# An attention and mixture-of-experts kernel: nine first products of the last batch turned round, their result transposed by DMA, the output tile split, the order refitted

## The chip, the cores and the metric

The kernel runs on one core of one Trainium2 chip. The metric is the device time of one execution in microseconds; the kernel before takes 357.3 us, the median of three runs (356.98 to 357.76).

## The reference

Sliding-window attention with sink tokens feeds a dense mixture of four experts. Shapes: q, k and v are (4 batches, 8 heads, 768 tokens, 64); x has 3072 tokens of 512; w1 is (4, 512, 1024), w2 is (4, 1024, 512).

```python
keep = is_sink | in_window                 # 4 sinks, window 128
a = softmax(where(keep, q @ k.T / 8, -1e9))
x = (a @ v) as (tokens, heads * dim)
p = domain_probs / (domain_probs.sum(-1, keepdims=True) + 1e-09)
for e in range(E):
    h = np.maximum(x @ w1[e], 0.0)
    out += p[:, e:e + 1] * (h @ w2[e])
```

## The kernel before, in words

**Work and tiling.** Tokens are worked in groups g of 256, three to a batch b, twelve in all. Attention of a batch consists of scores (line 673), values (735) and a DMA transpose of the result to x with features on partitions (`xT`, issued from SP at line 775). The first product of a group and an expert, x times w1, is a *unit* (b, g, e). Its result, after ReLU and the gate p, is `H`, with hidden features on partitions. The second product, H times w2, gathers all four experts of a group in a PSUM accumulator (`emit_product`, line 1316).

**Seven products in place of eight.** Most units and all second products from the third group on use a scheme of seven half-size matrix products, P1 to P7, of sums and differences of quarter blocks. Sums of the weights are made once (`weight_form1`, `weight_form`), those of the tokens once for a group (`tokens`, line 1103, tile `T`), those of H once for a unit (`chore`, line 1235, tiles `S` and `H` itself). All of these are VectorE work.

**A fast unit** (`emit_fast`, line 1135) issues each of its seven products as 8 matmuls: a block of 128 x 128 of the weight form stands in the array and 128 tokens stream past it (line 1158). Three PSUM banks X, Y and V take them. ScalarE seeds Y with P1 (line 1204) and keeps P5 in SBUF as fp32 in the memory of one half of H (line 1217); VectorE adds twice (1211, 1226) and then gates the four quarters with ReLU times the gate (1191). As tokens lie along the free dimension there, the gate is a tile of 128 x 256 with the same row on all partitions, loaded by SP (`load_gate`, 457) in a ring of four buffers. A quarter goes to the second product directly, so H is complete when the four gates are done.

**What sets the order.** The kernel is unrolled by a planner that runs while it is built. It keeps a clock for each engine (`pe`, `act`, `dve`, `sp`, lines 113 to 219) and at each step picks, among the steps that are ready, the one of the lowest priority number (lines 1535 to 1564). Attention is 1.9 when due and 3 otherwise, a pair of scores 0.1 less, an open unit's next product 2, opening a second unit OPEN, a second product LOW_PRODUCT. At most WIDE = 2 units are open. `SHARE_OF` spreads a batch's attention over the work of the batches before. Evacuations are queued with a slack (`later`, 152), and the one with the earliest due time goes first; "any" lets ScalarE or VectorE take it, whichever is free first. `joins` (1546) keeps a new unit from opening while a pair of scores is due and at least HOLDS units are open. `widened` (975) gives three more H buffers out of qkT once all attention is done. Each engine runs its instructions in the planner's order and waits on semaphores for what isn't ready.

**The output tile.** `emit_product` collects a group's result in one tile `osb` of two halves of 128 tokens, with one buffer; each half goes to memory by a DMA of its own (lines 1383 and 1324). Late groups alternate between it and two `aT` buffers.

Of the kernel before, what the change touches and what calls it, by code (L numbers as in the profile page):

```python
# [9 lines left out]
ALU = mybir.AluOpType  # L10
# [6 lines left out]
def kernel(  # L17
# [40 lines left out]
    ]  # L58

    NGATE = 4  # L60
    FIRST = 1
    START = {0: (1, 0), 1: (0, 2), 2: (0, 0), 3: (1, 0)}
    MIX = 6
    SHARE_OF = (0.9, 0.79, 0.98)
    LEAD = (1.01, 1.0)
    DUE = 1.9
    LOW_PRODUCT = 2.3
    LOW_SECOND = 2.7
    HIGH_PRODUCT = 1.9
    EARLY = -0.01  # L70
    MASK = 4000
    GATE = 1500
    GATE0 = 900
    FORM = 6000
    TOKEN = 5000
    MARGIN = 0
    HOLD = 0
    FULL = 7
    STEP0 = 0.01
    READY = 40  # L80
    WIDE = 2
    OPEN = 2.2
    SOON = 34000
    NEARLY = 2
    ROWED = 24000
    GATED = 38000
# [1 line left out]
    ROWS1 = 1500  # L88
    ONACT = 1
    ONE = 2  # L90
    HOLDS = 1
    MORE = 2
    BOTH = 1
    PAIR = 0
    OVER = 4
    ALONE = 1.3
    BEHIND = 1500
    CHORES = 3
    BIASED = 1
    FAST = tuple(START)  # L100
    BZ = 0
# [45 lines left out]
    def take(i, until):  # L147
        ring[i] = until
# [299 lines left out]

    def load_gates():

        while len(gate_sb) < len(mix.order) and (
            len(gate_sb) < (NGATE if t["pe"] > GATED else FIRST) or mix.order[len(gate_sb) - NGATE] in mix.finished
        ):
            b, g, e = mix.order[len(gate_sb)]
            load_gate(b * NG + g, e)

    def load_gate(pair, e):
# [480 lines left out]
    class Mixture:  # L938


        def __init__(self):
            self.early = {g: list(range(E)) for g in range(NEARLY)}
            self.open = []
            self.units = []
            for b, g in PAIRS:
                fast = [e for e in range(E) if self.is_fast(b, g, e)]
                slow = [e for e in range(E) if e not in fast]
                if b == 0:
                    fast, slow = list(range(E)), []
                while fast or slow:  # L950
                    for x in (fast, slow):
                        if x:
                            self.units.append((b, g, x.pop(0)))
            self.order = list(self.units)
            self.T, self.T_at, self.fast, self.finished = {}, {}, {}, set()
            self.second, self.live, self.since, self.turn, self.credit = [], 0, 0, 0, 0.0
            self.H, self.H_at, self.H_part = {}, {}, {}
            self.S, self.S_at, self.waiting, self.last = {}, {}, [], []
            self.products = [(b, g, m) for b, g in PAIRS for m in CHAIN]
            self.piece, self.part, self.chores = 0, 0, 0  # L960
            self.at, self.S4_at, self.C22 = {}, {}, {}
            self.done = 0.0
            self.stored, self.homed = [], False
            self.spare, self.lent = [], {}

# [4 lines left out]
            return bool(self.open or any(self.early.values()) or self.units or self.second or self.products)  # L970

        def room(self):
            return self.spare or self.live < NH

        def widened(self):

            x = sb.tile([P, 2, NHP, S], BF16, name="qkT", tag="qkT", bufs=1)
            x = x.rearrange("p i h n -> p (i h n)")
            n = 2 * QF * 2 * P
            self.spare = [x[:, i * n:(i + 1) * n].rearrange("p (k f t n) -> p k f t n", k=2, f=QF, t=2) for i in range(3)]  # L980

        def opened(self, b, g, e):

            if self.spare:
                self.H[b, g, e] = self.spare.pop()
                self.lent[b, g, e] = self.H[b, g, e]
            else:
                self.H[b, g, e] = mo.tile([P, 2, QF, 2, P], BF16, name="H", tag="H", bufs=NH)
                self.live += 1
            fast = self.is_fast(b, g, e)  # L990

            def complete(at):
# [141 lines left out]

        def emit_fast(self, u, m, ready):
            b, g, e = u["unit"]
            H, part, at = self.H[b, g, e], self.H_part[b, g, e], u["at"]
            if m == "P1":
                spare = [i for i in range(6) if ring[i] <= ready + 40]
# [92 lines left out]
            else:  # L1232
                u["last"](end)

        def chore(self):
# [24 lines left out]
            b, g, e = u = self.waiting[0]  # L1260
            if any(x[:2] < (b, g) and x[2] == "P5" for x in self.products) or any(x[:2] < (b, g) for x in self.last):
                return False
            if (b, g) == PAIRS[0] and (len(self.stored) < 2 * NEARLY or self.stored[-1] > t["pe"] + 500):
                return False
            self.waiting.pop(0)
            if (b, g) not in self.S:
                self.S[b, g] = [mo.tile([P, E, QF, P], BF16, name=f"S{i}", tag=f"wide{i}", bufs=1) for i in range(2)]
            H = self.H[b, g, e]
            H11, H21, H22 = H[:, 0, :, 0], H[:, 0, :, 1], H[:, 1, :, 1]
            S = self.S[b, g]  # L1270
            steps = [(nc.vector.tensor_add, S[0][:, e], H21, H22), (nc.vector.tensor_sub, S[1][:, e], S[0][:, e], H11),
                     (nc.vector.tensor_sub, H21, H11, H21)]
# [43 lines left out]
        def emit_product(self):  # L1316
# [40 lines left out]
            if m == "P1":  # L1357
                late = not att.more() and ahead == B - 1
                if late and self.homed:
                    x2 = [sb.tile([P, 2, 4 * P], BF16, name="aT", tag="aT", bufs=4) for _ in range(2)]  # L1360
                    out_sb[b, g] = [i.rearrange("p h w -> p (h w)").bitcast(FP32) for i in x2]
                else:
                    x2 = mo.tile([P, 2, Dout], FP32, name="osb", tag="osb", bufs=1)
                    out_sb[b, g] = [x2[:, i] for i in range(2)]
                self.homed = late and not self.homed
                self.C22[b, g] = join(2, lambda at: store(at))
            o = out_sb[b, g]
# [41 lines left out]
        def emit_second(self):  # L1409
            ready = self.second_ready()  # L1410
            g, s, e = self.second.pop(0)
            if g not in out_sb:
                out_sb[g] = mo.tile([P, 2, Dout], FP32, name="osb0", tag=f"wide{g}" if g < 2 else "osb", bufs=1)
                if g == 0:
                    gates()
            dst = out_sb[g][:, s]
# [32 lines left out]
                    used.add(e)  # L1449

    idle_products(acc[1], 9)
    mix = Mixture()
# [26 lines left out]
    while mix.more() or att.more():  # L1481
# [46 lines left out]
            next_form()  # L1528
        if ahead + 1 < B and not att.more() and (ahead == 0 or (ahead + 1, 0) in turned_at) and (ahead == 0 or mix.done >= sum(work[:ahead]) * LEAD[ahead - 1]):
            ahead += 1  # L1530
            att = Attention(ahead)
            upto = mix.done
        share = (sum(work[:ahead]) - upto) * SHARE_OF[max(ahead - 1, 0)]
# [8 lines left out]
                opts.append((max(r, now), p, "att", step))  # L1542
        s2, p = mix.second_ready(), mix.product_ready()
        behind = max(t["dve"] - now, 0.0) + 500 * sum(x[2] == "dve" and x[0] < now + 300 for x in pend)
        opts.append((max(p, now), HIGH_PRODUCT if behind > BEHIND or mix.live >= FULL else LOW_PRODUCT, "product", None))
        joins = due and ahead >= PAIR and att.two() and not late and len(mix.open) >= HOLDS
        opts += [(max(f, now), p, "first", x) for f, p, x in mix.firsts() if not (joins and x[0] in ("unit", "early"))]
        opts.append((max(s2, now), 1 if mix.since >= 1 else LOW_SECOND, "second", None))
# [14 lines left out]
            continue  # L1563
        r, _, kind, step = min(opts, key=lambda o: (o[0] > now + 40, o[0] if o[0] > now + 40 else 0, o[1]))
        assert r < 1e11
        if kind == "att":
            att.emit(step)
        elif kind == "first":
# [41 lines left out]
```

## Time and profile before

| | before |
|---|---|
| time, median of 3 runs | 357.3 us (356.98 to 357.76) |
| the profiled execution's own time | 357.25 us |
| its span | 355.5 us |
| granted TensorE clock, mean | 0.998 |
| TensorE busy | 349.7 us, 4563 matmuls |
| VectorE busy | 305.9 us, 704 instructions |
| ScalarE busy | 165.2 us, 423 instructions |
| first products of fast units, L1158 | 2240 matmuls of 128 columns |
| second products, L1335 | some 1100 matmuls, most of 256 columns |

The profile is of one execution. The span runs from the first to the last instruction. PE is TensorE, PEld its weight loads, DVE VectorE, ACT ScalarE, POOL GpSimd, SP the engine that issues most DMAs. A line number with L is a line of the kernel before; `cps` are the PSUM banks of fast units, `acc` the accumulators of second products, `sps` the banks of scores. Matmuls overlap, and their listed length (219 ns for 128 columns) is longer than the distance between two starts.

### The profile page before, as it was taken

Reading aid. Unit: us, or ns where it says so; the run is one execution under the profiler, and the core shown is the slowest. Engines: PE = TensorE matmul, PEld = TensorE weight load, DVE = VectorE, ACT = ScalarE, POOL = GpSimd, SP = SyncE. Lnnn points to the kernel's source line nnn. Section 1 sums busy time; section 2 is a strip of 40 time slices with the busy share of each in tenths; the row PEclk is TensorE's granted clock in tenths of the full one; section 3 lists DMA queues with packets and bytes.
Section 4 is the critical chain, followed back from the end, with each engine's and each line's share of the span. In section 5 each row is a group of like instructions: output and inputs, shape, how many; then the busy total and the mean of one; then the engine's idle time right before and its main releaser. Section 6 shows DMA issues by size and latency. Waiting matters only on the chain.

```text
span 355.5 us, 10875 instructions
## 1 busy us (share of the span) xinstructions
PE 349.7 (98%) x4563; PEld 302.4 (85%) x4563; DVE 305.9 (86%) x704; ACT 165.2 (46%) x423; POOL 73.6 (21%) x91
## 2 busy tenths in 40 slices
PE   8999999999999999999999999999999999999996
PEld 3685769656789998998998999899899999999985
DVE  5885999978999999799698998799899899899740
ACT  5863724447884565554542345455464223322111
POOL 8955114230534306010340000000000000000000
PEclk9999999999999999999999999999999999999999
DMA  9999999999999999629999120310210211010011
GB/s 176 178 187 196 222 216 181 170 153 180 150 144 157 177 153 117 78 64 72 160 144 160 46 57 21 77 50 21 77 50 19 52 56 61 31 44 33 1 61 60
DMA packets 120125, 37.80 MB, mean 106 GB/s; under 512 B 101268, under 2 KB 116084, under 8 KB 120076
## 3 DMA queue, kind: packets, MB, share of 16 engines
q0 software_dynamic: 79104, 17.31, 57.7%
q1 hardware_dynamic: 39916, 19.28, 27.5%
q8 instruction: 35, 0.57, 0.7%
q10 hardware_dynamic: 1056, 0.52, 0.5%
q14 instruction: 14, 0.11, 0.1%
HBM read 40.98 MB, written 6.34 MB: 133 GB/s over the span
## 4 chain that ended last, share of the span: by engine, by line
PE 93%; DVE 3%; DMA 2%; ACT 1%; issue 0%; ACTq 0%; DVEq 0%
PE cps L1158 35%; PE acc L1335 33%; PE acc L1422 8%; PE hps L1071 7%; PE sps L692 3%; PE od L758 3%; DMA out_dram<-osb 2%; PE acc L568 1%; PE od L751 1%; DVE onat L788 1%; DVE aT L726 1%; PE tx L816 0%; DVE T L1127 0%; PE tr L589 0%; PE sinks L653 0%; ACT aT L717 0%
## 5 line engine op out<-in xcount | busy, mean ns | idle before, releaser
L1158 PEld LDWEIGHTS <-w 128*128 128x128 bf16 x1280 | 78.7, 98 | 2.9 <-issue 1.3
L1335 PEld LDWEIGHTS <-H 128*128 128x128 bf16 x684 | 63.5, 98 | 7.3 <-issue 1.1
L1191 DVE SCALAR_TENSOR_TENSOR H<-cps,gates 128x512 bf16<-128x512 f32 x96 | 64.1, 678 | 0.1
L1158 PEld LDWEIGHTS <-vf 128*128 128x128 bf16 x960 | 58.4, 98 | 1.0 <-issue 0.3
L717 ACT ACTIVATE aT<-sps 128x512 bf16<-128x512 f32 (+1 forms) x96 | 47.2, 574 | 16.6 <-PE sps L692 16.5
L1335 PE MATMUL acc<-w,H 128*128 128x256 bf16 x408 | 53.9, 273 | 0.0
L1158 PE MATMUL cps<-T,w 128*128 128x128 bf16 x640 | 48.9, 219 | 0.0
L1158 PE MATMUL cps<-xT,w 128*128 128x128 bf16 x640 | 47.6, 219 | 0.0
L1158 PE MATMUL cps<-T,vf 128*128 128x128 bf16 x640 | 46.2, 219 | 0.0
L797 ACT ACTIVATE onat<-od,R 128x64 bf16<-128x64 f32 x144 | 33.2, 320 | 21.2 <-DVE R L785 21.0
L1204 ACT COPY cps<-cps 128x512 f32<-128x512 f32 x40 | 23.2, 579 | 41.1 <-PE cps L1158 22.1
L1397 ACT COPY osb<-acc 128x256 f32<-128x256 f32 x35 | 13.1, 377 | 50.9 <-PE acc L1335 46.1
L1335 PEld LDWEIGHTS <-S 128*128 128x128 bf16 x320 | 30.1, 98 | 4.2 <-issue 1.0
L1071 PE MATMUL hps<-xT,w 128*128 128x256 bf16 x256 | 31.8, 273 | 0.1
L1211 DVE TENSOR_TENSOR cps<-H,cps 128x512 f32<-128x512 f32 x34 | 23.4, 689 | 8.3 <-PE cps L1158 4.3
L1422 PE MATMUL acc<-w,H 128*128 128x512 bf16 x128 | 29.9, 379 | 0.0
L305 POOL DMA_DIRECT2D vx<-in_v_dram x24 | 21.4, 908 | 39.6 <-PE od L758 28.9
L1335 PE MATMUL acc<-wf,H 128*128 128x256 bf16 (+1 forms) x208 | 28.4, 272 | 0.0
L1071 PEld LDWEIGHTS <-w 128*128 128x128 bf16 x256 | 24.2, 98 | 4.5 <-issue 0.7
L1226 DVE TENSOR_TENSOR H<-H,cps 128x512 f32<-128x512 f32 x34 | 23.1, 679 | 2.2 <-PE cps L1158 2.1
L1158 PE MATMUL cps<-xT,vf 128*128 128x128 bf16 x320 | 24.4, 219 | 0.0
L240 POOL DMA_DIRECT2D qkn<-in_q_dram x22 | 19.6, 893 | 22.3 <-DMA qkT<-qkn 14.7
(127 smaller groups left out, 526.7 us busy)
## 6 DMA issues: line engine op xcount, KB each, us to landing
w<-in_moe_w_dram POOLq DMA_DIRECT2D x6, 1024.0 KB, 18.5
out_dram<-osb SPq DMA_DIRECT2D x21, 256.0 KB
gates<-gate_rows SPq DMA_DIRECT2D x40, 128.0 KB
vx<-in_v_dram POOLq DMA_DIRECT2D x24, 128.0 KB, 7.7
qkn<-in_q_dram POOLq DMA_DIRECT2D x22, 128.0 KB, 6.9
qkn<-in_k_dram POOLq DMA_DIRECT2D x22, 128.0 KB, 7.1
w<-in_moe_w_dram POOLq DMA_DIRECT2D x4, 256.0 KB, 7.3
w<-in_moe_w_dram POOLq DMA_DIRECT2D x2, 512.0 KB, 11.0
```

Of the source, the lines that this page charges most:

```text
L240: nc.gpsimd.dma_start(out=both[:, i], in_=src[b, :, tb * P:(tb + 1) * P, :].rearrange("h p d -> p h d"),)
L305: nc.gpsimd.dma_start(out=vx[tb][:, :, 0:D], in_=v[b, :, tb * P:(tb + 1) * P, :].rearrange("h p d -> p h d"),)
L717: nc.scalar.activation(out=a[:, ph], in_=sps[ph][:, 0:w], func=AF.Exp, scale=scale)
L797: nc.scalar.mul(o[:, qi, hp, ph * D:(ph + 1) * D], od[:, qi, ph, 0:D], R[:, qi, ph])
L1071: nc.tensor.matmul(h[:, i].rearrange("p (q n) -> p q n", q=2), lhsT=w1_sb[e][:, db, fb * P:(fb + 1) * P], rhs=xT[b, g][:, :, db], start=(i ...
L1158: nc.tensor.matmul(y[:, f], lhsT=A[:, d, f * P:(f + 1) * P], rhs=T[:, d], start=(m in ("P1", "P5") and f == 0 and d == 0), stop=(d == 1), ...
L1191: nc.vector.scalar_tensor_tensor(out=dst, in0=src, scalar=0.0, in1=gate, op0=ALU.max, op1=ALU.mult)
L1204: nc.scalar.copy(out=tiles["Y"], in_=y)
L1211: nc.vector.tensor_add(tiles["V"], c5, tiles["X"])
L1226: nc.vector.tensor_add(c5, c5, y)
L1335: nc.tensor.matmul(y, lhsT=self.operand(b, g, e, m)[:, f], rhs=forms[e][m][:, f, cs], start=(k == 0 and f == 0 and m in (("P1", "P5", "P2" ...
L1422: nc.tensor.matmul(op, lhsT=H[:, fb // QF, fb % QF, s], rhs=w2_sb[e][:, fb, :], start=(fb == 0), stop=(fb == NFB - 1),)
```

## The change

Nine of the twelve units of the last batch, all but its first two and its last, are *turning*. Their tokens stand in the array and the weight form streams past, so each of the seven products is 2 matmuls of 512 columns and the result has tokens on partitions. The gate is then a scalar per partition: VectorE applies ReLU and gate in one instruction with a pointer operand, or ScalarE does it in two. Results go to half-buffers of 128 x 1024 bf16, and a DMA transpose from SP turns each into its half of H, two for a unit. Six half-buffers are taken from tiles that attention no longer needs, so turning units open only after attention's end. Gate tiles for these units are no longer loaded; a small table of the last batch's gates (128 x 6 x 4) is loaded and normalized once. The output tile becomes two tiles. The experts of the last group come in another order, and constants of the planner change.

```diff
+    TURN_ABOUT = 0
+    TURNED_UNITS = (2, 1)
+    EXPERTS = {(2, 2): (2, 0, 3, 1)}
-    SHARE_OF = (0.9, 0.79, 0.98)
+    SHARE_OF = (0.96, 0.92, 0.94)
-    LOW_PRODUCT = 2.3
+    LOW_PRODUCT = 2.7
-    MASK = 4000
-    GATE = 1500
-    GATE0 = 900
-    FORM = 6000
-    TOKEN = 5000
+    MASK = 5000
+    GATE = 800
+    GATE0 = 300
+    FORM = 8000
+    TOKEN = 3000
+    REST = 1500
+    LANDS = 0
-    OPEN = 2.2
-    SOON = 34000
+    OPEN = 2.5
+    SOON = 28000
-    HOLDS = 1
+    HOLDS = 2
-    CHORES = 3
+    CHORES = 4
...
+            mine = [u for u in self.order if u[0] == B - 1]
+            self.turning = set(mine[TURNED_UNITS[0]:len(mine) - TURNED_UNITS[1]])
+            self.gated = [u for u in self.order if u not in self.turning]
...
         def room(self):
+            if self.units and self.units[0] in self.turning and self.halves() < 2:
+                return False
             return self.spare or self.live < NH
...
+            for tag, bufs, n in (("qkn", NQB, 3), ("onat", 2, 2), ("aT", 4, 1)):
+                self.resting += [(t["pe"], sb.tile([P, QF, 2, P], BF16, name="rest", tag=tag, bufs=bufs)) for _ in range(n)]
...
+        def emit_turning(self, u, m, ready):
...
+                    def turned(k):
+                        def turn(at):
+                            nc.sync.dma_start(
+                                out=H[:, k].rearrange("c f t n -> c (f t) n"), in_=X[k].rearrange("p f t n -> p (f t n)"), transpose=True,
+                            )
+                            done = sp(at, issue=1330, takes=1400, turning=True) + LANDS
+                            self.H_part[b, g, e](done)
+                            self.H_part[b, g, e](done)
+                            self.resting.append((done, X[k]))
+                        return join(2, turn)
...
+            for d in range(2):
+                nc.tensor.matmul(
+                    y.rearrange("p f n -> p (f n)"), lhsT=T[:, d], rhs=A[:, d], start=(m in ("P1", "P5") and d == 0), stop=(d == 1), skip_group_check=True,
+                )
+            end = pe(2 * n, ready, n=2)
...
+            def gated(k, s, src, ready, slack, slot=None, then=None):
+                gate = own_gates[:, 2 * g + s, e:e + 1]
+
+                def run(engine):
+                    if engine == "act":
+                        nc.scalar.activation(out=src, in_=src, func=AF.Relu)
+                        act(n)
+                        nc.scalar.mul(X[k][:, :, s], src, gate)
+                        at = act(n)
+                    else:
+                        nc.vector.tensor_scalar(out=X[k][:, :, s], in0=src, scalar1=0.0, scalar2=gate, op0=ALU.max, op1=ALU.mult)
+                        at = dve(n, fixed=152)
...
+                later("any" if slot is not None else "dve", ready, slack, run)
...
+            if u in self.turning and self.H_at[u] > max(t["pe"], t["dve"]):
+                return False
...
-                    x2 = mo.tile([P, 2, Dout], FP32, name="osb", tag="osb", bufs=1)
-                    out_sb[b, g] = [x2[:, i] for i in range(2)]
+                    out_sb[b, g] = [mo.tile([P, Dout], FP32, name=f"osb{i}", tag=f"osb{i}", bufs=1) for i in range(2)]
...
+            if ahead == B - 2:
+                own_load()
+            elif ahead == B - 1:
+                own_made()
...
-        opts.append((max(p, now), HIGH_PRODUCT if behind > BEHIND or mix.live >= FULL else LOW_PRODUCT, "product", None))
+        opts.append((max(p, now), HIGH_PRODUCT if behind > BEHIND or mix.live >= FULL or wide and TURN_ABOUT and mix.turn_about else LOW_PRODUCT, "product", None))
```

`own_load` issues one DMA for the gate table, and `own_made` four small VectorE steps that normalize it. The seeds, the two additions and the banks of a turning unit are those of `emit_fast`; three of its four gates may go to ScalarE, and the fourth, whose source is the fp32 copy in SBUF, stays on VectorE.

More of the change, by code (lines that the diff above doesn't have):

```diff
@@ L449, in load_gates @@
     def load_gates():
-        while len(gate_sb) < len(mix.order) and (
-            len(gate_sb) < (NGATE if t["pe"] > GATED else FIRST) or mix.order[len(gate_sb) - NGATE] in mix.finished
+        while len(gate_sb) < len(mix.gated) and (
+            len(gate_sb) < (NGATE if t["pe"] > GATED else FIRST) or mix.gated[len(gate_sb) - NGATE] in mix.finished
         ):
-            b, g, e = mix.order[len(gate_sb)]
+            b, g, e = mix.gated[len(gate_sb)]
             load_gate(b * NG + g, e)
@@ L945, in __init__ @@
             for b, g in PAIRS:
-                fast = [e for e in range(E) if self.is_fast(b, g, e)]
+                fast = [e for e in EXPERTS.get((b, g), range(E)) if self.is_fast(b, g, e)]
                 slow = [e for e in range(E) if e not in fast]
@@ L954, in __init__ @@
             self.order = list(self.units)
+            mine = [u for u in self.order if u[0] == B - 1]
+            self.turning = set(mine[TURNED_UNITS[0]:len(mine) - TURNED_UNITS[1]])
+            self.gated = [u for u in self.order if u not in self.turning]
+            self.G, self.resting = {}, []
             self.T, self.T_at, self.fast, self.finished = {}, {}, {}, set()
@@ L961, in __init__ @@
             self.at, self.S4_at, self.C22 = {}, {}, {}
-            self.done = 0.0
+            self.done, self.turn_about = 0.0, False
             self.stored, self.homed = [], False
@@ L972, in room, with halves, half @@
         def room(self):
+            if self.units and self.units[0] in self.turning and self.halves() < 2:
+                return False
             return self.spare or self.live < NH
+        def halves(self):
+            return sum(x[0] <= t["pe"] + REST for x in self.resting)
+        def half(self):
+            return self.resting.pop(min(range(len(self.resting)), key=lambda i: self.resting[i][0]))[1]
         def widened(self):
@@ L990, in opened @@
             fast = self.is_fast(b, g, e)
+            if (b, g, e) in self.turning:
+                self.G[b, g, e] = [self.half(), self.half()]
             def complete(at):
@@ L1136, in emit_fast @@
             b, g, e = u["unit"]
+            if (b, g, e) in self.turning:
+                self.emit_turning(u, m, ready)
+                return
             H, part, at = self.H[b, g, e], self.H_part[b, g, e], u["at"]
@@ L1233, in emit_fast, with seed, both, run @@
                 u["last"](end)
+        def emit_turning(self, u, m, ready):
+            b, g, e = u["unit"]
+            H, X, at = self.H[b, g, e], self.G[b, g, e], u["at"]
+            n = QF * P
+            assert len(own_steps) == 4
+            if m in ("P1", "P5"):
+                spare = [i for i in range(6) if ring[i] <= ready + 40]
+                spare.sort(key=lambda i: (whole[i], ring[i]))
+                if m == "P1":
+                    assert len(spare) >= 2
+                    new = dict(X=spare[0], Y=spare[-1])
+                    u["unset"] = not whole[spare[-1]]
+                    u["slots"], u["tiles"] = {}, {}
+                    def turned(k):
[8 more added lines that the diff above has]
+                        return join(2, turn)
+                    u["turn"] = [turned(k) for k in range(2)]
+                else:
+                    new = dict(V=spare[0])
+                for name, i in new.items():
+                    u["slots"][name] = i
+                    u["tiles"][name] = bank(i, [P, QF, P], FP32, "cps", True)
+                    ring[i] = 1e12
+            slots, tiles = u["slots"], u["tiles"]
+            y = tiles[{"P1": "X", "P5": "V", "P6": "X", "P2": "Y", "P7": "X", "P3": "V", "P4": "X"}[m]]
+            A, T = forms1[e][m], self.T[b, g][m]
+            for d in range(2):
[3 more added lines that the diff above has]
+            end = pe(2 * n, ready, n=2)
+            self.done += 2 * n
+            if m == "P1" and u["unset"]:
+                w = w1_sb[e][:, 0]
+                nc.tensor.matmul(
+                    tiles["Y"].rearrange("p f n -> p (f n)"), lhsT=w[:, 0:P], rhs=w[:, 0:n], start=True, stop=True,
+                )
+                pe(n)
+            c5 = X[1].rearrange("p f t n -> p (f t n)").bitcast(FP32).rearrange("p (f n) -> p f n", f=QF)
+            def gated(k, s, src, ready, slack, slot=None, then=None):
[6 more added lines that the diff above has]
+                        at = act(n)
+                    else:
+                        nc.vector.tensor_scalar(out=X[k][:, :, s], in0=src, scalar1=0.0, scalar2=gate, op0=ALU.max, op1=ALU.mult)
+                        at = dve(n, fixed=152)
+                    if slot is not None:
+                        take(slot, at)
+                    u["turn"][k](at)
+                    if then:
+                        then(at)
+                later("any" if slot is not None else "dve", ready, slack, run)
+            if m == "P1":
+                u["last"] = join(2, lambda at: gated(1, 1, tiles["X"], at, GATE, slots["X"]))
+                def seed(engine):
+                    nc.scalar.copy(out=tiles["Y"], in_=y)
+                    at["P6"] = at["P2"] = act(n)
+                later("act", end, 0, seed)
+                at["P5"] = self.T_at[b, g]
+                def both(ready):
+                    def run(engine):
+                        nc.vector.tensor_add(tiles["V"], c5, tiles["X"])
+                        at["P7"] = at["P3"] = dve(n)
+                    later("dve", ready, 0, run)
+                u["both"] = join(2, both)
+            elif m == "P5":
+                def keep(engine):
+                    nc.scalar.copy(out=c5, in_=y)
+                    u["both"](act(n))
+                later("act", end, 0, keep)
+            elif m == "P6":
+                u["both"](end)
+            elif m == "P2":
+                gated(0, 1, y, end, GATE, slots["Y"])
+            elif m == "P7":
+                def run(engine):
+                    nc.vector.tensor_add(c5, c5, y)
+                    at["P4"] = dve(n)
+                    gated(1, 0, c5, at["P4"], 100, then=u["last"])
+                later("dve", end, 0, run)
+            elif m == "P3":
+                gated(0, 0, y, end, GATE, slots["V"])
+            else:
+                u["last"](end)
@@ L1412, in emit_second @@
             if g not in out_sb:
-                out_sb[g] = mo.tile([P, 2, Dout], FP32, name="osb0", tag=f"wide{g}" if g < 2 else "osb", bufs=1)
+                out_sb[g] = mo.tile([P, 2, Dout], FP32, name="osbw", tag=f"wide{g}", bufs=1)
                 if g == 0:
@@ L1449, in emit_second, with own_load, own_made, run @@
                     used.add(e)
+    own_gates = consts.tile([P, 2 * NG, E], FP32, name="own_gates")
+    own_sum = consts.tile([P, 2 * NG], FP32, name="own_sum")
+    own_steps = []
+    def own_load():
+        nc.sync.dma_start(out=own_gates, in_=moe_domain_probs[(B - 1) * S:].rearrange("(t p) e -> p t e", p=P))
+        sp()
+    def own_made():
+        steps = [
+            lambda: nc.vector.reduce_sum(out=own_sum, in_=own_gates, axis=AX.X),
+            lambda: nc.vector.tensor_scalar_add(out=own_sum, in0=own_sum, scalar1=1e-9),
+            lambda: nc.vector.reciprocal(out=own_sum, in_=own_sum),
+            lambda: nc.vector.tensor_mul(own_gates, own_gates, own_sum[:, :, None].to_broadcast([P, 2 * NG, E])),
+        ]
+        def run(engine):
+            steps.pop(0)()
+            dve(2 * NG * E)
+            own_steps.append(1)
+            if steps:
+                later("dve", t["dve"], 5000, run)
+        later("dve", t["pe"], 5000, run)
     idle_products(acc[1], 9)
@@ L1565 @@
         assert r < 1e11
+        mix.turn_about = kind == "first"
         if kind == "att":
```

## The prediction

> **What bounds the kernel now.** I read the shares of the page first, then the chain of waits in order of time, then the table of stretches, and last the timeline at the places where the chain leaves TensorE.
>
> ```profile
> PE 349.7 (98%) x4563; PEld 302.4 (85%) x4563; DVE 305.9 (86%) x704; ACT 165.2 (46%) x423; POOL 73.6 (21%) x91
> ...
> PE 93%; DVE 3%; DMA 2%; ACT 1%; issue 0%; ACTq 0%; DVEq 0%
> ```
>
> TensorE carries 93% of the chain that ended last. A busy PE may still hide waiting, so I took the spacing of matmul starts from unbroken pieces of the chain (start, length, what):
>
> ```profile
> 26.45 5.18 PE acc L1422 x24
> ...
> 304.63 5.36 PE cps L1158 x96
> ...
> 311.75 5.24 PE acc L1335 x48
> ...
> 331.19 20.11 PE acc L1335 x192
> ```
>
> 24 matmuls of 512 columns take 5.18 us, 0.216 each; 96 of 128 columns take 5.36 us, 0.0559 each; 48 of 256 take 5.24 us, 0.109 each. Setting every start in the trace against the spacing of its shape leaves 11.8 us that TensorE did not use: 6.2 us before 60 us, 5.6 us after it. From 280 us on there is none.
>
> ```profile
> 280.00:300.00 20.00, 20.00 (x294) 19.22 (x293) 19.63 (x42) 5.41 (x11) 0.00 (x0) 1.00 0.16 54
> 300.00:320.00 20.00, 20.00 (x274) 18.96 (x272) 18.38 (x39) 4.84 (x10) 0.00 (x0) 1.00 0.12 34
> ...
> 340.00:356.00 16.00, 12.19 (x128) 10.95 (x125) 2.69 (x7) 2.23 (x7) 0.00 (x0) 0.94 0.17 63
> ```
>
> The columns are PE, PEld, DVE, ACT, POOL, granted clock, DMA share and GB/s. Where the last batch runs, VectorE is nearly full too, ScalarE and the DMA engines are nearly free, and at the end VectorE has long stopped while TensorE works on. So only fewer TensorE nanoseconds, or fewer of the 11.8 us, shorten this kernel.
>
> **The turned products.** A product of a normal unit is 8 matmuls of 128 columns, 8 x 55.9 = 447 ns. A turned one is 2 of 512, 2 x 216 = 432 ns. Saved: 15.2 ns a product; 9 units of 7 products are 63, so **0.96 us**, all on the bounding engine. The weight loads fall from 8 to 2, but they are hidden already: 96 matmuls with as many loads start every 55.9 ns though one load is listed at 98 ns.
>
> The Trainium skill ("TensorE: Matmul & The Clock Gate", section on the back-to-back issue gap) gives a sustained spacing of about 81 ns at 128 columns and 131 ns at 512 in streams with weight loads. By it a product would fall from 648 to 262 ns and the change would win some 24 us; the chain above contradicts both figures.
>
> **VectorE and ScalarE.** The 36 gating instructions of these units leave their old form. Rows for the old and the new ones (busy, mean ns):
>
> ```profile
> L1191 DVE SCALAR_TENSOR_TENSOR H<-cps,gates 128x512 bf16<-128x512 f32 x96 | 64.1, 678 | 0.1
> ...
> L1086 DVE TENSOR_SCALAR H<-hps 128x512 bf16<-128x512 f32 x5 | 3.4, 685 | 0.5 <-PE hps L1071 0.4
> ...
> L1432 DVE TENSOR_SCALAR osb<-acc,scale_t 128x512 f32<-128x512 f32 x4 | 3.0, 750 | 3.4 <-PE acc L1422 3.4
> ```
>
> A scalar per partition seems to cost 65 ns (750 against 685), at most 36 x 0.07 = 2.5 us of VectorE. Against that, 27 of the 36 may go to ScalarE as two instructions of about 0.6 us each (606 for the ReLU of L1084, 579 for the copy of L1204): up to 27 x 0.60 = 16 us less VectorE, where 0.60 is its spacing in a row of such gates. ScalarE is a quarter busy there, so the cover is ample. I cost both at nothing, because TensorE has no wait from 280 us on and cannot have fewer than none. Without the cover, up to 2.5 us of VectorE work would be spread over a stretch with 2.0 us of VectorE idle (40 - 19.63 - 18.38), and 20 us of pure second products behind it would still absorb it. The four steps for the new gates on VectorE are tiny (0.16 to 0.18 us each by L925 and L928), and 24 numbers a partition are loaded some 100 us before use; nothing.
>
> **The DMAs.** Added are 18 transposes from SP, removed 9 gate loads. SP is held 1.24 us by a transpose (L775, 1237 ns undisturbed), so 22 us in some 55 us of queue; stores and the last gate loads stand behind them. From issue to the last landing record the undisturbed xT transposes, of the same 128 x 1024 size, took 3.03 us (221 us) and 3.08 us (250 us), and 3.66 us behind a gate load (275 us). The planner's book counts 1.33 + 0.8 + 1.4 + 0.9 = 4.43 us. A transposed half is thus ready 0.8 to 1.4 us ahead of plan; cost nothing. What waits for it is the second product on TensorE and the sums for P5 to P7 on VectorE. Each engine takes its instructions in the program's order, so a late landing would hold everything behind it on that engine. Under the heavier traffic of 159 to 190 us the same transposes took 5.3 to 8.3 us, the upper bound.
>
> The Trainium skill ("VectorE: DVE Perf Modes", section on the three transpose paths) lists 1309 ns for a 128 x 128 DMA transpose. Eight blocks one after another would be 10.5 us, twice the plan; the 3.03 us rows speak against it.
>
> **The output tile.** One stall in the chain is a copy that waits for a store of the same tile:
>
> ```profile
> 190.54 0.60 PE L1335 MATMUL acc<-qkn,S 128*128 128x256 bf16 x4
> ...
> 191.06 0.65 ACT L1397 COPY osb<-acc 128x256 f32<-128x256 f32 x2 [4.75 <-DMA out_dram<-osb]
> ...
> 191.48 0.60 PE L1335 MATMUL acc<-w,S 128*128 128x256 bf16 x4 [0.34 <-ACT osb L1397]
> ```
>
> Four matmuls end their slots at 190.54 + 0.44 = 190.98; the next starts at 191.48. The store was the second half's (L1324, 184.03, landed 6.99 us later); the copy writes the first half, whose store had landed long before. Two tiles remove that wait: **0.50 us**. Nothing else is late behind it: the timeline shows no wait of TensorE in the next microseconds.
>
> **The refitted order.** LOW_PRODUCT (2.3 to 2.7) and OPEN (2.2 to 2.5) keep their rank against each other and against the other priorities that can compete, so they change nothing. CHORES and the slacks reorder VectorE, whose order costs TensorE nothing after 280 us; before, I take zero with bounds. TOKEN acts early: four T steps hold 1.68 us of the chain at 14.7 to 16.5 us, so up to 0.7 us either way. SHARE_OF moves attention; what is lost after 60 us besides shape switches is about 1.2 us, the bound on both sides.
>
> HOLDS from 1 to 2 is more than a tuning. It kept a second unit from opening while a pair of scores was due; units open only while fewer than two are open, so at 2 the reservation never acts. A pair needs four free banks of six. What a lone group costs:
>
> ```profile
> 263.58 0.60 PE L1335 MATMUL acc<-w,H 128*128 128x256 bf16 x4
> ...
> 264.11 0.62 PE L692 MATMUL sps<-qkT 64*128 64x128 bf16 x12
> ...
> 264.66 0.62 PE L1158 MATMUL cps<-T,w 128*128 128x128 bf16 x8
> ```
>
> 264.11 is 0.09 us past the slots of the four before it, and another 0.09 follows the group: 0.19 us for each separate group. After 76 us there are 23 groups, some 12 of them pairs. Splitting none costs nothing, splitting all 12 costs 2.3 us. I take 2 (0.38 us), near the lower end: a ready pair still outranks a new unit (1.8 against 2.5), and pairs such as 264.11 stand where the open units were nearly done.
>
> **The sum.** On the profiled execution (357.25 us, span 355.5 and 1.7 around it; 0.05 below the median of 357.3): 357.25 - 0.96 - 0.50 + 0.38 = 356.17, so **356.2 us**.
>
> **Rivals.** *The forecast as worked out*, 355.3 to 356.8: 0.46. *The new order also recovers stalls* (1.2 us after 60 us, some of the 6.2 before): 354.2 to 355.3; for it, VectorE gains room; against it, TensorE waits for VectorE only early, where the new gates are not yet used: 0.16. *The pairs of scores come apart*, 6 to 12 of them: 357.25 - 1.46 + 1.1 to 2.3 = 356.9 to 358.1; for it, the reservation is gone and units fill banks; against it, the rank above: 0.20, mostly within 0.2%. *The turned halves come late*, the one on the slower side: each unit's first use stalls TensorE in order. It decides from 4.43 us after the gating; with 0.5 us of lateness for each of 9 units, 356.2 + 4.5 = 360.7, and slower than before from 0.2 us each. For it, two more hops (ScalarE, SP); against it, 0.8 to 1.4 us of reserve by the rows: 0.12. *The change does not do what it says*: half-buffers exist only once attention is done, so a third unit waiting for them, or early reshuffling, eats the gain (357 to 358.5). Before, the third unit of the last batch starts at 276.1 and the last attention transpose at 275.23, so there is little to wait for: 0.05. *Weight loads bind, not columns*: at 98 ns a matmul of 128 columns a turned unit would save 7 x (784 - 432) ns, 22 us in all, so 335; the 55.9 ns rows exclude it nearly: 0.01. The Trainium skill's spacing rule above points this way.
>
> **Numbers.** This kernel's measurement tells about 0.2% (0.7 us) from no change. Faster: 0.42 + 0.16 + 0.01 = 0.59. Within: 0.04 + 0.15 + 0.02 + 0.02 = 0.23. Slower: 0.05 (pairs) + 0.10 (late) + 0.03 = 0.18. The range runs from 354.4 to 358.4 and leaves out most of the late rival and the lowest tail.
>
> **What would show it.** Right: 126 matmuls of 512 columns at 0.216 us in place of 504; no copy of L1397 waiting on a store; transposes landing 3.0 to 3.7 us after issue; no gap on TensorE after 280 us; 23 to 26 groups of scores after 76 us. Wrong: TensorE or VectorE waiting for H from DMA (late halves); over 30 groups (pairs); a third unit well after attention's end. A gain over 2 us would mean that the early stalls moved.

## The result and the profile after

| | before | after |
|---|---|---|
| time, median of 6 runs each | 357.14 us | 355.08 us (355.03 to 355.93) |
| ratio | | 0.9947, 95% interval 0.9933 to 0.9962 |
| profiled execution, its span | 357.25, 355.5 us | 355.08, 353.1 us |
| first to last matmul | 350.56 us | 348.63 us |

Two later repeats gave 2.23 us less (0.9935, 0.9922 to 0.9949) and 2.08 us less (0.9938, 0.9922 to 0.9955). The forecast was 356.2, 1.05 us less: right in sign, the result inside the range, the gain about half of what was measured.

The page after, the shares of the engines and the head of its chain:

```profile
PE 347.8 (98%) x4184; PEld 286.2 (81%) x4184; DVE 295.9 (84%) x690; ACT 185.9 (53%) x459; POOL 73.7 (21%) x91
...
PE 94%; DVE 2%; DMA 2%; ACT 1%; issue 0%; ACTq 0%; DVEq 0%
```

There are 379 fewer matmuls: 504 of 128 columns became 126 of 512, and one more of 512 went, which before had cleared a bank (L1166). TensorE still bounds. The chain in order of time:

```profile
279.95 3.88 PE cps L1294 x18
...
327.41 21.96 PE acc L1463 x208
```

18 turned matmuls take 3.88 us, 0.2156 each, the spacing that L1422 had before. The stretches of the last batch:

```profile
280.00:300.00 20.00, 20.00 (x125) 12.10 (x124) 16.82 (x37) 15.28 (x29) 0.00 (x0) 1.00 0.62 112
300.00:320.00 20.00, 20.00 (x147) 14.19 (x146) 12.33 (x29) 11.86 (x22) 0.00 (x0) 1.00 0.53 113
```

The columns are those of the table of stretches in the prediction. VectorE fell from 38.0 to 29.2 us in these 40, ScalarE rose from 10.3 to 27.1, the DMA share from 0.14 to 0.58. The instructions on the half-buffers (columns: count, then minimum, median and maximum ns, first and last start):

```profile
L1314 ACT ACTIVATE rest<-cps,own_gates x18: 687/687/687, 278.0 to 323.1; 128x512 bf16<-128x512 f32 x18
...
L1275 SPq DMA_TRANSPOSE H<-rest x12: 1231/1262/1505, 287.5 to 321.7; - x12
...
L1317 DVE TENSOR_SCALAR rest<-rest,own_gates x9: 474/480/486, 279.8 to 322.8; 128x512 bf16<-128x512 f32 x9
L1317 DVE TENSOR_SCALAR rest<-cps,own_gates x9: 742/749/752, 280.4 to 323.9; 128x512 bf16<-128x512 f32 x9
```

Of 36 gates 18 went to ScalarE and 18 stayed on VectorE; a scalar per partition costs 64 ns on a PSUM source (749 against 685), as the prediction took it. On ScalarE a gate takes two instructions, L1312 for ReLU and L1314 for the gate.

**How the variants are compared.** The variants were timed in three series (the expectations name a series a call), each with the kernel before beside them. Device times of one kernel scatter by 0.1 to 1.9 us within a series, as much as the parts in question. A sharper measure is the *stream*: the time from the first matmul start to the last, less the filler products and gaps of the first 24 us, which vary from run to run with what lands when (9.8 to 10.3 us). For three executions of the changed kernel, one from the result and two from later series, it is 338.61, 338.61 and 338.62 us. The figure of every other kernel but t4_noturn is from one execution, and it moves by up to 0.06 us with the way the early gaps are counted. Some traces lack records of 512-column matmuls; such places show as gaps of 216 ns more than the spacing, with the weight load on record, and are not counted as waits.

| kernel | stream, us | median against before in its series, us | ratio to before, 95% |
|---|---|---|---|
| before | 340.72 | | |
| t1_tile | 340.11 | -0.96 | 0.9974, 0.9964 to 0.9984 |
| t2_order | 339.41 | -2.05 | 0.9941, 0.9928 to 0.9955 |
| t3_turn | 340.19 | -0.87 | 0.9981, 0.9971 to 0.9991 |
| t4_noturn, t4b_noturn | 339.39, 339.40 | -1.83, -1.57 | 0.9951, 0.9939 to 0.9964; 0.9953, 0.9939 to 0.9968 |
| after, a0_after, a1_after | 338.61, 338.61, 338.62 | -2.06, -2.23, -2.08 | given above |
| e5_cols128 | 339.55 | -1.38 | 0.9958, 0.9945 to 0.9970 |
| e6_onetile | 338.67 | -2.10 | 0.9943, 0.9926 to 0.9960 |
| e8_dvegates | 338.54 | -2.44 | 0.9931, 0.9918 to 0.9943 |
| e9_lands | 339.06 | -1.93 | 0.9946, 0.9929 to 0.9963 |
| e10_turn_dve | 339.65 | -0.82 | 0.9971, 0.9961 to 0.9982 |

### The profile page after: what moved, and what is told of

It reads as the page before. It is cut to its first block, busy times and chain, and to the rows that moved or that the text cites. A ratio compares the mean times of both kernels' runs of the same rounds, so it can differ in the third digit from the quotient of the medians.

```text
span 353.1 us, 10221 instructions
## 1 busy us (share of the span) xinstructions
PE 347.8 (98%) x4184; PEld 286.2 (81%) x4184; DVE 295.9 (84%) x690; ACT 185.9 (53%) x459; POOL 73.7 (21%) x91
## 4 chain that ended last, share of the span: by engine, by line
PE 94%; DVE 2%; DMA 2%; ACT 1%; issue 0%; ACTq 0%; DVEq 0%
PE acc L1463 35%; PE cps L1182 28%; PE acc L1549 8%; PE cps L1294 8%; PE hps L1092 7%; PE sps L697 3%; PE od L763 3%; DMA kraw<-in_k_dram 2%; PE od L756 1%; DVE aT L731 1%; DVE onat L793 1%; PE tx L821 1%; PE tr L594 0%; DVE T L1148 0%; PE sinks L658 0%; ACT aT L722 0%
## 5 line engine op out<-in xcount | busy, mean ns | idle before, releaser
L1463 PEld LDWEIGHTS <-H 128*128 128x128 bf16 x708 | 65.4, 98 | 9.2 <-issue 1.6
L1182 PEld LDWEIGHTS <-w 128*128 128x128 bf16 x992 | 61.5, 98 | 2.3
L1215 DVE SCALAR_TENSOR_TENSOR H<-cps,gates 128x512 bf16<-128x512 f32 x81 | 54.3, 679 | 0.2
L1182 PEld LDWEIGHTS <-vf 128*128 128x128 bf16 x744 | 45.4, 98 | 1.9 <-issue 0.8
L1182 PE MATMUL cps<-T,w 128*128 128x128 bf16 x496 | 37.6, 219 | 0.0
L1182 PE MATMUL cps<-xT,w 128*128 128x128 bf16 x496 | 37.3, 219 | 0.0
L1182 PE MATMUL cps<-T,vf 128*128 128x128 bf16 x496 | 36.2, 219 | 0.0
L1228 ACT COPY cps<-cps 128x512 f32<-128x512 f32 x31 | 18.3, 589 | 21.8 <-PE cps L1182 8.4
L1092 PEld LDWEIGHTS <-w 128*128 128x128 bf16 x256 | 24.1, 98 | 4.6 <-issue 0.9
L1235 DVE TENSOR_TENSOR cps<-H,cps 128x512 f32<-128x512 f32 x29 | 20.0, 688 | 7.6 <-PE cps L1182 7.5
L716 DVE TENSOR_TENSOR aT<-aT,mask 128x1024 bf16<-128x1024 bf16 (+1 forms) x36 | 22.7, 636 | 1.4 <-ACT aT L722 1.3
L1549 PEld LDWEIGHTS <-H 128*128 128x128 bf16 x128 | 12.3, 98 | 12.2 <-issue 0.2
```

Source lines behind the costliest of these rows:

```text
L716: nc.vector.tensor_mul(a, a, m[:, None, :].to_broadcast([P, 2, w]))
L1092: nc.tensor.matmul(h[:, i].rearrange("p (q n) -> p q n", q=2), lhsT=w1_sb[e][:, db, fb * P:(fb + 1) * P], rhs=xT[b, g][:, :, db], start=(i ...
L1182: nc.tensor.matmul(y[:, f], lhsT=A[:, d, f * P:(f + 1) * P], rhs=T[:, d], start=(m in ("P1", "P5") and f == 0 and d == 0), stop=(d == 1), ...
L1215: nc.vector.scalar_tensor_tensor(out=dst, in0=src, scalar=0.0, in1=gate, op0=ALU.max, op1=ALU.mult)
L1235: nc.vector.tensor_add(tiles["V"], c5, tiles["X"])
L1463: nc.tensor.matmul(y, lhsT=self.operand(b, g, e, m)[:, f], rhs=forms[e][m][:, f, cs], start=(k == 0 and f == 0 and m in (("P1", "P5", "P2" ...
```

## The experiments

**First series: each part of the change alone, and the change without its main part.**

*The output tile alone*, on the kernel before (the edit also renames the tile of the first two groups, and nothing else):

```diff
-                    x2 = mo.tile([P, 2, Dout], FP32, name="osb", tag="osb", bufs=1)
-                    out_sb[b, g] = [x2[:, i] for i in range(2)]
+                    out_sb[b, g] = [mo.tile([P, Dout], FP32, name=f"osb{i}", tag=f"osb{i}", bufs=1) for i in range(2)]
```

> The kernel before with the output tile in two tiles and nothing else. Theory A (the gain is a sum of separate parts: 0.96 us of matmul spacing, 0.5 us of the output tile, the rest from waits that the new order avoids): the copy that waits for a store at 191 us is gone and the matmul stream is 0.50 us shorter, so 0.5 us less than before (0.14%). Rival B (the refitted order makes nearly all of the 2 us, its parts alone nothing): 0.0 us, another wait takes the place of this one.

The stream is 0.61 us shorter, as Theory A has it and not Rival B. The 502 ns gap at 190.9 us is gone, and so is one of 0.17 us at 278.6; a copy of the stretch at 191 us waits for TensorE alone:

```profile
191.53 0.37 ACT L1396 COPY osb<-acc 128x256 f32<-128x256 f32 x1 [1.82 <-PE acc L1335]
```

The time says 0.57 to 1.29 us by its interval. That its middle, 0.96 us, is more than the stream's 0.61 may come from a longer wait in other executions of the kernel before; no profile shows one, so it stays open.

*The order alone*: the constants that both kernels have, put into the kernel before. The experts' order, which the expectation names, is not in this edit: its kernel has no `EXPERTS`.

```diff
-    SHARE_OF = (0.9, 0.79, 0.98)
+    SHARE_OF = (0.96, 0.92, 0.94)
...
-    HOLDS = 1
+    HOLDS = 2
...
```

> The kernel before with the refitted constants and the new order of experts, and nothing turned, one output tile. Theory A: waits of TensorE between 76 and 280 us fall by some 0.4 us beside the output tile's, so 0 to 0.7 us less than before. Rival B: 1.5 to 2 us less. Rival P (my prediction's term: without the reservation pairs of scores come apart): 0.4 us or more longer, with more than 23 groups of scores.

The stream is 1.31 us shorter and the time 2.05 us. Theory A's 0 to 0.7 is too small by both; Rival B's 1.5 to 2 fits the time and not the stream. Against the gaps of before: the 0.50 us at the output tile are gone although the tile is still one, other waits between 76 and 264 us fall by 0.24, the 0.17 after 264 us vanish, one group of scores fewer saves 0.19, and the clearing matmul is not needed (0.22). These make 1.32. Here is the copy of that stretch, with no wait before it:

```profile
190.39 0.39 ACT L1397 COPY osb<-acc 128x256 f32<-128x256 f32 x1
```

Rival P is refuted: groups of scores after 76 us are 22, one fewer than before. With HOLDS at 2 and the other constants moved along with it, the pairs did not come apart. HOLDS was not changed by itself.

*Turning and the tile with the old order*: the changed kernel, with all shared constants and the experts' order as before.

> The kernel after with all constants of before that both have, experts in the old order: nine units turned and the output tile in two, the order not refitted. Theory A: 0.96 + 0.5 us less than before, 1.2 to 1.7. Rival B: 0 to 0.5 us less, since the old constants bring waits of TensorE in the last batch. Rival D (transposed halves come late unless the order is fitted for them): longer than before, with TensorE or VectorE waiting for H from a DMA.

Between the two theories: 0.53 us of stream and 0.87 us of time. TensorE waits 0.97 us after 264 us, against 0.17 before. None of these waits ends with a DMA, and the kernel is not slower, so Rival D falls; one wait for a transposed half is on record, 1.33 us of VectorE at 293.3, with no gap on TensorE behind it. The timeline of this kernel shows the first of the larger waits:

```profile
285.87 0.59 ACT L1312 ACTIVATE cps<-cps 128x512 f32<-128x512 f32 x1
286.14 0.59 PE L1294 MATMUL cps<-w,T 128*128 128x512 bf16 x2
286.50 0.69 ACT L1314 ACTIVATE rest<-cps,own_gates 128x512 bf16<-128x512 f32 x1
...
287.01 0.60 PE L1463 MATMUL acc<-qkn,H 128*128 128x256 bf16 x4
287.08 0.59 ACT L1330 COPY cps<-cps 128x512 f32<-128x512 f32 x1
...
287.72 0.59 PE L1294 MATMUL cps<-vf,T 128*128 128x512 bf16 x2
```

P1 of the new unit is on TensorE from 286.14 to 286.73. Its seed (L1330) starts only at 287.08, behind both instructions of a gate of the other unit on ScalarE (L1312 and L1314). The product that needs the seed starts at 287.72; four matmuls before it fill 0.44 us, and 0.28 us are lost. A second seed, at 304.89, costs 0.31 us in the same way, and 0.18 us at 298.8 end as a gate on ScalarE ends (L1314). Of the rest, 0.17 us stand at the last unit, which is not turned; the changed kernel has the same two waits (further down).

*The changed kernel with nothing turned*:

```diff
-    TURNED_UNITS = (2, 1)
+    TURNED_UNITS = (12, 0)
```

> The kernel after with no unit turned: refitted order and two output tiles alone. Theory A: 1.0 to 1.2 us more than after, so 0.8 to 1.0 us less than before. Rival B: as after, 2 us less than before. Rival C (the work moved from VectorE to ScalarE is what pays): 1.5 us or more above after, with TensorE waiting for VectorE in the last batch.

By the time it is 1.83 us less than before, outside Theory A's 0.8 to 1.0 and near Rival B's 2. The stream is 0.78 us above the changed kernel, and that fits 0.96 of spacing less 0.17 us of waits that stand after 264 us in the changed kernel and not here. Those two waits are at the last unit of the batch. The first ends with an addition on VectorE, the second with a copy between accumulators on ScalarE, both of which had themselves just waited for TensorE:

```profile
326.06 0.69 DVE L1250 TENSOR_TENSOR qkT<-qkT,cps 128x512 f32<-128x512 f32 x1 [0.26 <-PE cps L1182]
...
326.80 0.61 PE L1182 MATMUL cps<-T,w 128*128 128x128 bf16 x8
326.94 0.36 ACT L1502 COPY acc<-acc 128x256 f32<-128x256 f32 x1 [2.63 <-PE acc L1463]
...
327.35 1.91 PE L1463 MATMUL acc<-w,H 128*128 128x256 bf16 x16
```

ScalarE had been idle for 2.63 us, so no gate stood in front of that copy. Beside the constants alone, the second tile and the experts' order together bring nothing (339.39 against 339.41). As time and stream disagree on what turning is worth, the next two series measure it again.

**Second series: the disputed cost by itself, and which engine takes the gates.**

> The changed kernel once more, beside its variants on one chip. Theory A' (by the matmul streams: the refitted order saves 1.3 us, of it 0.5 at the output tile, which the second tile alone also saves; the turned products add 0.96 less 0.2 of new waits): 2.1 us less than before and 0.8 us less than the kernel without turning. Rival B (order alone, turning nothing): as that kernel, 1.8 us less than before, within 0.2.

355.21 us, 2.23 less than before, and the stream 2.11 less: Theory A' fits, and the time lies outside Rival B's 1.6 to 2.0.

*Turned units as 8 matmuls of 128 columns*, the planner's books as they were:

```diff
-                nc.tensor.matmul(
-                    y.rearrange("p f n -> p (f n)"), lhsT=T[:, d], rhs=A[:, d], start=(m in ("P1", "P5") and d == 0), stop=(d == 1), skip_group_check=True,
-                )
+                for f in range(QF):
+                    nc.tensor.matmul(
+                        y[:, f], lhsT=T[:, d], rhs=A[:, d, f * P:(f + 1) * P], start=(m in ("P1", "P5") and d == 0 and f == 0), stop=(d == 1), skip_group_check=True,
+                    )
```

> The changed kernel with each turned product as 8 matmuls of 128 columns and 8 weight loads in place of 2 of 512; the planner's books and so the order are as in the changed kernel. Theory A': 63 x 15.2 ns = 0.96 us more matmul stream, less at most the 0.2 us of late waits, so 0.8 to 0.96 us more than the changed kernel. Rival B: no difference. Rival W (weight loads cost time when the tokens stand): more than 1.5 us.

0.85 us more time than a0_after, 0.93 us more stream. The same nine products that took 3.88 us at 279.95 in the changed kernel:

```profile
280.00 4.02 PE cps L1295 x72
```

0.14 us for nine is 15.6 ns a product, with four times the matmuls and four times the weight loads, and no further loss. So fewer and wider matmuls gain about 2.6 ns for each of the six that a product saves; Rival W, that each load costs time of its own, falls. Whether these 2.6 ns belong to the matmul or to its load can't be told apart here, as both fell together.

*All gates on VectorE*:

```diff
-                later("any" if slot is not None else "dve", ready, slack, run)
+                later("dve", ready, slack, run)
```

> The changed kernel with all 36 gates of the turned units on VectorE, none on ScalarE. Theory A' (VectorE has room, TensorE bounds): within 0.3 us of the changed kernel. Rival C (the relief of VectorE pays): 1 us or more longer, TensorE waits for VectorE between 276 and 330 us.

355.00 against 355.21 us, stream 338.54 against 338.61: no difference the time can tell. Its stretches:

```profile
280.00:300.00 20.00, 19.89 (x130) 12.75 (x131) 18.97 (x40) 5.40 (x11) 0.00 (x0) 1.00 0.50 106
300.00:320.00 20.00, 19.89 (x134) 13.16 (x135) 18.80 (x41) 5.42 (x11) 0.00 (x0) 1.00 0.62 119
```

VectorE carries 37.8 of 40 us again and TensorE does not wait in these stretches (the missing 0.1 us in each are records that this trace lacks); one wait of 0.09 us, for an addition on VectorE, stands behind them at 320.4. Rival C falls: moving some 9 us from VectorE to ScalarE gains nothing.

*The same edit with the old order*:

> Turned units and two output tiles with the old constants, as in t3_turn, but all gates on VectorE. In t3_turn TensorE lost 1.0 us after 264 us. Theory S (a seed of the next unit stands on ScalarE behind two-instruction gates of the one before): that falls to 0.2 us or less, 0.8 us less than t3_turn. Rival D (DMA landings): the 1.0 us stays.

Half a miss. The waits after 264 us fell from 0.97 to 0.39 us and the stream by 0.54 us, so ScalarE's gates did cost in t3_turn. But one wait of 0.39 us stays, and by the time nothing is resolved: 0.82 us less than before, against 0.87 in t3_turn. The wait that stays is again for a seed, but no gate stands before it; ScalarE had been idle until P1 came, and only one other product lay between P1 and the one that needs the seed:

```profile
294.92 0.57 ACT L1330 COPY cps<-cps 128x512 f32<-128x512 f32 x1 [2.66 <-PE cps L1294]
...
295.54 0.38 PE L1294 MATMUL cps<-vf,T 128*128 128x512 bf16 x1 [0.23 <-ACT cps L1330]
```

This profiled execution also had its last stores land 0.8 us later than in the others (2.86 us after the last matmul's start, against 2.09).

**Third series: turning again on one chip, the tile, and late halves.**

> The changed kernel a third time, as the measure for the others of this call: 2.0 to 2.3 us less than before. Its comparison with the kernel without turning decides between Theory A' (turning is worth 0.78 us by the streams) and Rival B (turning is worth nothing, within 0.2 us).

> The refitted order and two output tiles with no unit turned, again, beside the changed kernel on the same chip. Theory A': 0.6 to 0.9 us longer than the changed kernel. Rival B: within 0.2 us of it.

355.35 and 355.86 us: 0.51 us by the time, 0.78 by the stream. Every run of the changed kernel here was faster than every run without turning, so Rival B (within 0.2) falls. The time misses the lower bound of Theory A', 0.6, and the stream is inside. So turning gains 0.5 to 0.8 us on top of the new order, and the order makes the larger part.

*The changed kernel with one output tile* (the edit of t1_tile backwards):

> The changed kernel with its output tile in one piece again. Theory O (the refitted order has moved the copy so that the store has landed, and the second tile is of no more use): within 0.2 us of the changed kernel, no copy on ScalarE waits for a store for longer than TensorE has other work. Rival T (the tile is worth its 0.5 us in any order): 0.5 us or more longer.

355.33 against 355.35 us, the stream the same to 0.06, and no wait of a copy for a store. Theory O holds: in the new order the tile is not needed.

*Halves that come later than planned*: the planner books them 2.4 us earlier than in the changed kernel.

```diff
-    LANDS = 0
+    LANDS = -2400
```

> The changed kernel with the planner's book for a turned half 2.4 us shorter (2.0 us after the gating in place of 4.4), while the transposes take 3.0 us as before: each half comes 1.0 us late against the plan. Rival D's mechanism (late halves stall in-order engines at each unit): up to 9 us longer, 3 us or more if a third of the units are hit. Theory R (second products are booked well after their halves and other work lies between): within 0.5 us of the changed kernel.

355.50 us, 0.15 more, not resolved; stream 0.44 longer, with two new gaps of 0.26 and 0.20 us at 292.3 and 295.2. The first ends as a gate on ScalarE ends, the second with an addition on VectorE, neither with a DMA. One wait for a transposed half is on record, on VectorE up to 291.5, while TensorE had other products:

```profile
DVE S L1404 <- DMA qkT<-rest: 2.3, 1, 2.3
```

Theory R holds. With halves booked some 1 us too early the cost is at most half a microsecond, not the 3 to 9 us of Rival D. Whether the two gaps follow from VectorE's wait or from the order, which this edit also moves, is not shown.

## Why the prediction was right in sign and short in size

- **The bound.** Right. TensorE holds 94% of the chain after, and some 9 us of work moved back to VectorE changed nothing.
- **The turned products, 0.96 us.** Right, and the mechanism too: 0.93 us of stream and 0.85 us of time when only the width is taken back. The step left out that turning adds waits of its own. With the old order they are some 0.8 us, most of it from ScalarE's two-instruction gates ahead of a seed. With the new order they are 0.17 us at the last unit, where no gate is in the way. I had costed the gates on ScalarE at nothing because that engine was a quarter busy; its share said nothing of what stands behind an instruction in its queue. That the changed kernel doesn't pay for this is the new order's doing and not the prediction's.
- **VectorE and pointer operands.** Right: 64 ns more on each PSUM source, hidden.
- **The DMAs.** Right. In the changed kernel 15 of the 18 transposes landed 3.0 to 3.3 us after issue, and three took 4.0 to 4.7, in a row of transposes or behind a store. The plan held 4.43, the one of 4.67 made nothing wait, and even a plan of 2.03 did little harm. The upper bound of 5.3 to 8.3 us mixed in transposes of q and k: the two of xT in that stretch took 6.2 and 6.7 us. That late halves would stall each unit was too dear a rival.
- **The output tile, 0.50 us.** Right for the old order (0.57 to 1.29 us by the time); but the new order avoids the same wait, so the two terms are not a sum, and in the changed kernel the tile is worth nothing measurable.
- **The refitted order, +0.38 us. This step failed.** I took "2 (0.38 us)" pairs lost and zero for the rest. One group of scores was saved instead, and the constants made the stream 1.31 us shorter by themselves. The rank argument for LOW_PRODUCT and OPEN was not tested alone. What I called a bound, 1.2 us after 60 us, was real and mostly won, the output tile's wait among it. Which of the constants did it is open; they were not tried one by one. That the experts' order adds nothing is shown only with nothing turned.
- **The sum.** Against 1.46 - 0.38 = 1.08 us foreseen, the stream fell 2.11: 1.31 by the order, the tile's wait included, and 0.78 by turning with its waits; the remaining 0.02 is within the scatter of these figures. The sum was too small by 1.03 us: the order was off by 1.69 us (+0.38 against -1.31), and in the other direction stand the tile's 0.50 us, which the order also wins, and 0.17 us of new waits. That the result lies inside the range is owed in part to these errors being of opposite sign. The span of the profiled executions fell by more than the stream, 2.42 us: 0.49 more at the program's end (last section), 0.18 less in the first 24 us. How much of the 0.49 is in the measured time is not shown, so the agreement of 2.11 us of stream with 2.06 us of time is partly luck.

The rival "recovers stalls" (354.2 to 355.3, chance 0.16) is the one that came true, together with the forecast's own term for turning. Its reason, room on VectorE from turning, is not what did it: the constants won the stalls with nothing turned. And its counter-argument, that TensorE waits for VectorE only early, misread the trace of before: the 0.17 us at 278.6, in the last batch, end with an addition on VectorE (L1211).

## What to carry to other kernels

Where one engine is nearly full, count its gaps in the trace one by one, sort them by cause, and treat a refitted order as able to win the avoidable ones; a reading of one constant's meaning was a poorer guide than that list. Two edits that remove the same wait do not add up. Before work goes to an engine with a low share, ask what stands behind it in that engine's queue and who waits for it.

## What the runs showed of the hardware

The program's end took a different time in different kernels, and no edit was meant to change it. From the start of the last matmul to the end of the span it took 3.55 us before and 3.06 us in all three profiled executions of the changed kernel, though the last store landed 2.09 and 2.08 us after that start. SP then waits for its semaphores one after another. Before, the last store's semaphore has three more behind it in this list, and 0.60 us pass to the drain, with one step of 0.39 us; after, it is the last but one, and 0.13 us pass. t2_order with 3.21 us and t4_noturn with 3.12 us lie between. Why the one step took 0.39 us is not shown. The span is some 0.5 us shorter by it; whether the times carry it was not tried by itself.

A change between the 64-row tiles of the scores and full tiles costs 0.092 to 0.096 us each way in every kernel here.
